# One eight-bank PSUM tile in place of four two-bank tiles, in a kernel with a fixed order of operations

## The chip, the cores and the metric

The kernel runs on one core of one Trainium2 chip. The metric is the device time of one execution in microseconds (us), the median over several executions. A run counts as slow when it is over 1.5% above the fastest of its kernel. The others are called fast, and only those enter ratios. Medians and the ranges behind them are over all runs, slow ones too.

Words used below: PE is the matrix engine, ACT the scalar engine, DVE the vector engine, POOL the general-purpose engine, SP the engine that issues most loads. PSUM is the memory that PE writes its results to; this kernel uses all of it, as eight banks of 512 fp32 values per partition. ACT and DVE empty ("evacuate") those banks.

## The reference

```python
# attention over 8 batches x 8 heads, 576 positions, head size 64
scores = q @ k.T / sqrt(64)          # heads 0-3: the last 32 positions; heads 4-7: every 4th of the last 128
attn   = softmax(where(mask, scores, -1e9)) @ v
x      = heads side by side          # [8, 576, 512]
# channel mix
x_prev = x shifted by one position
xk, xr = mu_k*x + (1-mu_k)*x_prev,  mu_r*x + (1-mu_r)*x_prev
k      = relu(xk @ w_k)              # [.., 1024]
out    = sigmoid(xr @ w_r) * (k*k @ w_v)
```

All inputs and the output are float32; the kernel computes in fp16 with fp32 sums in PSUM.

## The kernel before

The kernel plans itself in Python. It lists its operations (one operation is, for example, the four matmuls of one accumulation), simulates them with rough costs, and records the order that came out. Each engine then runs that fixed order. The planner also assigns the PSUM banks, and it takes the eight banks as independent of each other:

```python
P = Plan(pools, {"pa": OPTIONS["pa"], "p1": OPTIONS["p1"], "cm": OPTIONS["cm"], ...})
OPTIONS = dict(..., pa=[(0, 1), (2, 3), (4, 5)],    # attention: scores and outputs, a pair of banks each
               p1=[(0,), (1,), (2,), (3,)],         # attention: transposes, one bank each
               cm=[(4,), (5,), (6,), (7,)], ...)    # channel mix: one bank for each accumulation
```

The planner does not write semaphores. A layer below it looks at which tiles an instruction reads and writes and puts in the waits. What it sees of PSUM is this:

```python
PA = many(4, [128, 2, 512], FP32, "PA", psp)        # four tiles of two banks

def first(x):
    return P.cells[x.pool][x.idx][0][1]             # number of the first bank that the planner chose

def bank(x):
    return PA[first(x) // 2][:, first(x) % 2]

def banks(x):
    return PA[first(x) // 2]
```

Two parts of the channel mix (cut):

```python
# pk_ops: k = relu(xk @ w_k), one 128-wide slice f at a time, in one bank pk of pool "cm"
nc.tensor.matmul(out=o, lhsT=wk[:, c, f * 128:f * 128 + 128], rhs=XK[:, c, :, a0:a0 + 128],   # L801, 4 of these
                 start=(c == 0), stop=(c == 3))
nc.scalar.activation(out=KR[...], in_=view(), func=AF.Relu, scale=0.5 ** 0.5)                 # L805, evacuates pk
nc.vector.tensor_tensor(out=K2[...], in0=KR[...], in1=KR[...], op=ALU.mult)                   # L815
...
# pv_ops: two more banks, pr and pv
nc.tensor.matmul(out=view(pr)[:, g], lhsT=XR[...], rhs=wr[:, c], ...)                         # L844, 4 of these
nc.scalar.activation(out=TH[...], in_=view(pr), func=AF.Tanh, scale=0.5)                      # L847, evacuates pr
nc.tensor.matmul(out=view(pv)[:, g], lhsT=K2[...], rhs=wv[:, f], ...)                         # L853, 2 times 4 of these
nc.vector.scalar_tensor_tensor(out=OT[...], in0=TH[...], scalar=1.0, in1=view(pv), ...)       # L857, evacuates pv
```

In the attention part, L494 and L522 are transposes of the inputs, L563 and L614 scores, L585 and L635 outputs, and L597, L647 and L704 transposes of the normalised outputs.

The softmax here doesn't subtract the row's maximum and nothing guards it: scores larger than these inputs give would overflow.

Of the kernel before, what the change touches and what calls it, by code (L numbers as in the profile page):

```python
# [9 lines left out]
FP32 = mybir.dt.float32  # L10
# [176 lines left out]
def kernel(  # L187
# [23 lines left out]
    psp = ctx.enter_context(tc.tile_pool(name="psp", bufs=1, space=PSUM))  # L211
# [7 lines left out]
    def many(n, shape, dt, name, pool=const):  # L219
        return [pool.tile(shape, dt, name=f"{name}{i}") for i in range(n)]  # L220
# [31 lines left out]
    M0 = const.tile([128, 8, 96], FP16, name="M0")  # L252
    MB = const.tile([128, 160], FP16, name="MB")
    MB0 = const.tile([128, 2, 96], FP16, name="MB0")
    PA = many(4, [128, 2, 512], FP32, "PA", psp)

    def buf(pool, turn=None):
        return Buf(pool, turn)
# [1 line left out]
    def first(x):  # L260
        return P.cells[x.pool][x.idx][0][1]

    def bank(x):
        return PA[first(x) // 2][:, first(x) % 2]

    def banks(x):
        return PA[first(x) // 2]


    def setup_pool():  # L270
# [22 lines left out]
    def mask_mm(ps, n, rhs):  # L293

        w = math.prod(rhs.shape[1:])
        for par in range(2):
            nc.tensor.matmul(out=banks(ps)[0:n, par, 0:w], lhsT=ident[:, 0:n], rhs=rhs, start=True, stop=False)  # L297
# [38 lines left out]
    def turn_mu():  # L336
        for i in range(2):
            nc.tensor.transpose(out=bank(mub)[:, 4 * i:4 * i + 4], in_=mu[:, i], identity=id4)

    def fix_mu():  # L340
        nc.vector.tensor_scalar(out=nm, in0=bank(mub)[:, 0:8], scalar1=-1.0, scalar2=None, op0=ALU.add)
# [126 lines left out]
    def attention(b, A):  # L468
# [16 lines left out]
        def pt(i, hp):  # L485
            pa = buf(one)

            def tv():
                return bank(pa).bitcast(FP16)[:, 0:576].rearrange("p (y x) -> p y x", y=9)

            def mm():
                for y in range(9):
                    for e in range(2):
                        nc.tensor.transpose(out=tv()[64 * e:64 * e + 64, y], in_=QP[bq.idx][64 * e:64 * e + 64, i, hp, 64 * y:64 * y + 64],  # L494
                                            identity=ident[64 * e:64 * e + 64, 64 * e:64 * e + 64], tile_position=(64 * e, 64 * e))

            m = P.op("PE", 9 * 0.038, mm, dep=[L["p", i], ident_op] + (XREADY[0][0][OPT['hold']] if b == 1 and OPT['hold'] is not None else []), use=[pa, bq, qt], prio=nxt(), warm=False)
            T = (QT, KT)[i]
            QTR[i, hp] = flex(576, ("ACT", "DVE") if b == 0 else ("ACT",),
                              lambda: T[qt.idx][:, hp, 32 * i:].rearrange("p (x y) -> p x y", y=9), lambda: tv().rearrange("p y x -> p x y"),  # L500
                              dep=[m], use=[pa, qt], prio=nxt())
# [44 lines left out]
        def view_o(g):  # L546
            return lambda po: banks(po)[:, 0:g, 0:260].rearrange("p w (h d) -> p w h d", d=65)

        def plain(j):
            ps, at = buf(two), buf("at")  # L550

            def s_mm():
                t = banks(ps)
                if pm:
                    mask_mm(ps, 128, (MB0 if j == 0 else MB[:, 32:128].unsqueeze(1).to_broadcast([128, 2, 96])).unsqueeze(2)
                            .to_broadcast([128, 2, 2, 96]))
                for wl in range(2):
                    w = 2 * j + wl
                    for hp in range(2):
                        for par in range(2):  # L560
                            e = par * 64
                            o = wl * 192 + hp * 96
                            nc.tensor.matmul(out=t[:, par, o:o + 96], lhsT=KT[qt.idx][e:e + 64, hp, 96 * w:96 * w + 128],  # L563
                                             rhs=QT[qt.idx][e:e + 64, hp, 96 * w:96 * w + 96],
                                             start=not pm, stop=not pm or wl + hp == 2)
# [322 lines left out]
    for b in range(1, B):  # L888
# [4 lines left out]
        def en(x):  # L893
            return {"P": ("POOL",), "D": ("DVE",), "A": ("ACT",), "*": ANY, "PA": ("POOL", "ACT"), "PD": ("POOL", "DVE")}[o["e" + x]]
        if o["p"]:
# [59 lines left out]
```

## Time and profile before

| | before |
|---|---|
| time when predicted | 273.19 us median of 3 (272.81 to 277.19) |
| span of the profiled run | 276.7 us (a slow run, granted clock 0.951) |
| PE / DVE / ACT / POOL busy | 238.7 / 182.2 / 153.8 / 74.2 us |
| 720 large matmuls, 215 ns apart when they stream | 155 us |

The page of the profile, its first and fourth part (busy times with shares of the span; the chain that ended last, by engine), and two lines of its fifth (busy time, mean length in ns, then idle time of PE just before and what ended most of it):

```profile
span 276.7 us, 6139 instructions
...
PE 238.7 (86%) x2442; PEld 123.7 (45%) x2442; DVE 182.2 (66%) x361; ACT 153.8 (56%) x255; POOL 74.2 (27%) x93
...
PE 68%; DVE 16%; ACT 9%; issue 3%; DMA 2%; SPq 0%; DVEq 0%; ACTq 0%
...
L801 PE MATMUL PA<-XK,wk 128*128 128x512 f16 x288 | 72.7, 392 | 7.0 <-ACT KR L805 3.9
L853 PE MATMUL PA<-wv,K 128*128 128x512 f16 x288 | 72.8, 389 | 6.7 <-ACT TH L847 4.0
```

No engine is full. PE leads, but "busy 86%" flatters it: the end of a matmul in the profile is modelled, and a large one is drawn as 379 ns long although the next starts 215 ns after it in a stream. For every matmul I take the time to the next one's start and subtract what is usual for its kind (the 20th percentile of its line). The sum of what is left is called PE's **standstill** here: 82.6 us in this run.

What PE and its two helpers wait for, from the view of waits (engine and instruction, then what it waited for: us in total, times, longest):

```profile
ACT KR L805 <- PE PA L801: 33.2, 42, 3.0
DVE K L815 <- ACT KR L805: 25.6, 23, 2.8
...
ACT TH L847 <- PE PA L844: 19.8, 13, 2.1
...
DVE OT L857 <- PE PA L853: 18.0, 13, 2.0
...
ACT TH L847 <- DVE OT L857: 9.6, 8, 2.7
ACT TH L847 <- PE PA L853: 7.5, 7, 2.1
...
DVE OT L857 <- PE PA L844: 4.3, 4, 1.6
...
PE PA L853 <- ACT TH L847: 4.0, 7, 0.7
PE PA L801 <- ACT KR L805: 3.9, 9, 0.7
```

Some of these lines are natural, at least in part: the relu L805 reads what L801 wrote. Others should surprise. The tanh L847 reads bank pr, which L844 wrote. It shares no data with L853, which writes pv, yet it waited 7.5 us for it. It waited 9.6 us for L857, and L853 in turn waited for the tanh. Such waits can be true: L857 reads what a tanh wrote, and there are only two TH buffers to write to; L853 may take over a bank that a tanh has emptied.

The timeline shows one such place closely (start, duration, engine, line, operation; in brackets the idle time before it and what ended that):

```profile
216.39 1.03 PE L801 MATMUL PA<-XK,wk 128*128 128x512 f16 x4
...
217.50 1.02 PE L801 MATMUL PA<-XK,wk 128*128 128x512 f16 x4
...
218.53 1.03 PE L801 MATMUL PA<-XK,wk 128*128 128x512 f16 x4
218.56 1.64 ACT L805 ACTIVATE KR<-PA 128x512 f16<-128x512 f32 x3 [2.70 <-PE PA L801]
```

The first four matmuls fill bank 7 and end at 217.42 (the banks are read from the built program). ACT is idle, and the relu of bank 7 takes 0.60 us, but it starts at 218.56, right after the *second* four end at 218.52, and those write bank 6. Three relus then run in a row. The built programs say why. They list, for each instruction, the semaphore values that it waits for; here the values are translated to the instructions that set them:

```
before  relu of bank 7 waits for: DVE L815 (its output buffer), the last matmul into bank 6
after   relu of bank 7 waits for: DVE L815 (its output buffer), the last matmul into bank 7
```

### The profile page before, as it was taken

What the parts mean: (1) busy time and instruction counts of PE and PEld (TensorE: products, weight loads), DVE (VectorE), ACT (ScalarE), POOL (GpSimd) and SP (SyncE); (2) the same over time, 40 slices, a digit from 0 to 9 for tenths busy, and PEclk for the clock granted to TensorE, in tenths of its full rate; (3) what the DMA queues carried; (4) which work ended last, traced back from release to release, by engine and by line L of the source; (5) the groups of instructions that cost most, each with busy time, mean ns of one, the idle gap of its engine ahead of it and who ended that gap; (6) DMA issues with size and microseconds to landing.
All of it is one profiled execution on the core that took longest, in us unless ns stands there. A gap on an engine that the chain in (4) does not pass through costs nothing.

```text
span 276.7 us, 6139 instructions
## 1 busy us (share of the span) xinstructions
PE 238.7 (86%) x2442; PEld 123.7 (45%) x2442; DVE 182.2 (66%) x361; ACT 153.8 (56%) x255; POOL 74.2 (27%) x93
## 2 busy tenths in 40 slices
PE   1967898699898889978699999978888999999993
PEld 1544255354454445435344455534433554444441
DVE  7676555886864869797657777967576887323221
ACT  2555477583566477667248664766476555644210
POOL 4022575363442317156222344320000000000000
PEclk9985599979999999999689999999999999999999
DMA  7999999999699989599837899861102022111231
GB/s 227 282 239 351 296 217 304 196 238 219 197 247 191 307 183 261 163 261 252 212 121 174 247 242 277 186 146 38 40 0 77 2 76 78 38 39 38 79 114 76
DMA packets 66397, 47.92 MB, mean 173 GB/s; under 512 B 40760, under 2 KB 57152, under 8 KB 66368
## 3 DMA queue, kind: packets, MB, share of 16 engines
q1 hardware_dynamic: 64784, 45.96, 66.3%
q0 software_dynamic: 1584, 1.57, 3.4%
q8 instruction: 19, 0.31, 0.5%
q14 instruction: 10, 0.08, 0.1%
HBM read 36.11 MB, written 9.44 MB: 165 GB/s over the span
## 4 chain that ended last, share of the span: by engine, by line
PE 68%; DVE 16%; ACT 9%; issue 3%; DMA 2%; SPq 0%; DVEq 0%; ACTq 0%
PE PA L853 22%; PE PA L801 21%; PE PA L844 10%; ACT KR L805 4%; DVE OT L857 3%; PE PA L494 3%; PE PA L297 3%; DVE XS L537 2%; PE PA L563 2%; ACT TH L847 2%; DMA ST<-in_q_dram 2%; DVE K L815 1%; DVE XT L350 1%; PE PA L597 1%; DVE AT L625 1%
## 5 line engine op out<-in xcount | busy, mean ns | idle before, releaser
L801 PE MATMUL PA<-XK,wk 128*128 128x512 f16 x288 | 72.7, 392 | 7.0 <-ACT KR L805 3.9
L853 PE MATMUL PA<-wv,K 128*128 128x512 f16 x288 | 72.8, 389 | 6.7 <-ACT TH L847 4.0
L805 ACT ACTIVATE KR<-PA 128x512 f16<-128x512 f32 x72 | 41.1, 597 | 38.6 <-PE PA L801 33.2
L857 DVE SCALAR_TENSOR_TENSOR OT<-TH,PA 128x512 f32<-128x512 f32 x36 | 24.7, 687 | 36.5 <-PE PA L853 18.0
L815 DVE TENSOR_TENSOR K<-KR 128x1024 f16<-128x1024 f16 x36 | 29.0, 808 | 25.6 <-ACT KR L805 25.6
L853 PEld LDWEIGHTS <-K 128*128 128x128 f16 x288 | 27.3, 99 | 38.9 <-issue 11.6
L847 ACT ACTIVATE TH<-PA 128x512 f32<-128x512 f32 x36 | 21.4, 596 | 39.7 <-PE PA L844 19.8
L801 PEld LDWEIGHTS <-wk 128*128 128x128 f16 x288 | 26.9, 99 | 36.8 <-issue 11.1
L844 PE MATMUL PA<-wr,XR 128*128 128x512 f16 x144 | 36.9, 379 | 0.1
L537 DVE TENSOR_TENSOR XS<-PA,RC 96x512 f16<-96x512 f32 (+2 forms) x48 | 30.9, 644 | 1.5
L348 POOL CAST QD<-ST 128x1024 f16<-128x1024 f32 (+1 forms) x21 | 19.8, 955 | 44.5 <-DMA ST<-in_k_dram 22.6
L348 POOL CAST VD<-ST 112x1024 f16<-112x1024 f32 (+1 forms) x16 | 18.0, 1134 | 17.8 <-DMA ST<-in_v_dram 16.3
L346 ACT ACTIVATE XT<-PA 128x384 f16<-128x384 f16 (+2 forms) x22 | 10.5, 486 | 19.2 <-PE PA L704 6.9
L348 POOL CAST QP<-ST 128x1152 f16<-128x1152 f32 x14 | 16.2, 1161 | 17.5 <-DMA ST<-in_q_dram 10.1
L568 ACT ACTIVATE AT<-PA 128x768 f16<-128x768 f32 x24 | 18.6, 811 | 4.2 <-PE PA L563 3.4
L494 PE MATMUL PA<-ident,QP 64*64 64x64 f16 x576 | 14.4, 206 | 7.1 <-DVE QP L350 5.8
L348 POOL CAST VP<-SV 128x512 f16<-128x512 f32 x21 | 14.0, 701 | 21.0 <-DMA SV<-in_v_dram 11.6
L844 PEld LDWEIGHTS <-XR 128*128 128x128 f16 x144 | 13.2, 98 | 14.1
L350 DVE COPY XT<-PA 128x384 f16<-128x384 f16 (+2 forms) x26 | 11.6, 449 | 10.9 <-PE PA L597 4.8
L494 PEld LDWEIGHTS <-QP 64*64 64x64 f16 x576 | 12.6, 120 | 11.3 <-DVE QP L350 5.9
L739 ACT ACTIVATE XR<-DX,nm 128x576 f16<-128x576 f16 (+2 forms) x23 | 15.5, 697 | 0.0
L533 DVE RECIPROCAL RC<-PA 96x8 f32<-96x8 f32 (+2 forms) x48 | 8.9, 185 | 9.8 <-PE PA L585 6.3
(77 smaller groups left out, 272.8 us busy)
## 6 DMA issues: line engine op xcount, KB each, us to landing
SV<-in_v_dram SPq DMA_DIRECT2D x8, 736.0 KB, 6.8
ST<-in_k_dram SPq DMA_DIRECT2D x8, 576.0 KB, 5.8
ST<-in_q_dram SPq DMA_DIRECT2D x8, 576.0 KB, 5.4
ST<-in_k_dram SPq DMA_DIRECT2D x8, 512.0 KB, 5.8
ST<-in_q_dram SPq DMA_DIRECT2D x8, 512.0 KB, 5.6
ST<-in_v_dram SPq DMA_DIRECT2D x8, 448.0 KB, 5.2
ST<-in_v_dram SPq DMA_DIRECT2D x8, 256.0 KB, 5.4
ST<-in_moe_w_k_dram SPq DMA_DIRECT2D x4, 512.0 KB, 6.8
```

The costliest lines, as they stand in the source:

```text
L348: nc.gpsimd.tensor_copy(out=o, in_=i)
L494: nc.tensor.transpose(out=tv()[64 * e:64 * e + 64, y], in_=QP[bq.idx][64 * e:64 * e + 64, i, hp, 64 * y:64 * y + 64], identity=ident[64 * ...
L537: nc.vector.tensor_tensor(out=XS[xs.idx][0:n, 0:g].rearrange("p w (h d) -> p w h d", h=4), in0=fin(po)[0:n, :, :, 0:64], in1=RC[rc.idx][0: ...
L568: nc.scalar.activation(out=AT[at.idx][:, :, 0:96].rearrange("p (a g) c -> p a g c", a=2), in_=banks(ps)[:, :, 0:384].rearrange("p a (g c) ...
L739: nc.scalar.activation(out=d, in_=x, func=AF.Copy, scale=mu[:, c:c + 1])
L801: nc.tensor.matmul(out=o, lhsT=wk[:, c, f * 128:f * 128 + 128], rhs=XK[:, c, :, a0:a0 + 128], start=(c == 0), stop=(c == 3))
L805: nc.scalar.activation(out=KR[kr.idx][:, g0:g0 + G], in_=view(), func=AF.Relu, scale=0.5 ** 0.5)
L815: nc.vector.tensor_tensor(out=K2[k2.idx][:, 2 * f2:2 * f2 + 2], in0=KR[kr.idx], in1=KR[kr.idx], op=ALU.mult)
L844: nc.tensor.matmul(out=view(pr)[:, g], lhsT=XR[:, c, rr[g], a:a + 128], rhs=wr[:, c], start=(c == 0), stop=(c == 3))
L847: nc.scalar.activation(out=TH[th.idx][:, 0:m], in_=view(pr), func=AF.Tanh, scale=0.5)
L853: nc.tensor.matmul(out=view(pv)[:, g], lhsT=K2[k2.idx][:, f, 128 * rr[g]:128 * rr[g] + 128], rhs=wv[:, f], start=(f == 0), stop=(f == NF - 1))
L857: nc.vector.scalar_tensor_tensor(out=OT[ot.idx][:, 0:m], in0=TH[th.idx][:, 0:m], scalar=1.0, in1=view(pv), op0=ALU.add, op1=ALU.mult)
```

## The change

The intent is to describe PSUM to the layer below as what it is, eight banks in one memory, without touching any operation, its place in the order or its bank.

```diff
-    PA = many(4, [128, 2, 512], FP32, "PA", psp)
+    PA = psp.tile([128, 8, 512], FP32, name="PA")
 ...
     def bank(x):
-        return PA[first(x) // 2][:, first(x) % 2]
+        return PA[:, first(x)]

     def banks(x):
-        return PA[first(x) // 2]
+        return PA[:, first(x):first(x) + 2]
```

That is all of it. The two programs have the same instructions in the same order on every engine; what differs is waits and the wait-only instructions that carry some of them.

## The prediction

> **What bounds the kernel.** PE's order of work. The chain of waits runs 68% through PE, 16% DVE, 9% ACT, 2% DMA. The 720 large matmuls start 215 ns apart when they stream (start times in the trace): 155 us of a 276.7 us span. The small matmuls take some 49 us (start-to-start times, summed). "PE busy 86%" counts modelled ends; by start times PE stands still for about 70 us. The page's DMA row is at 9 tenths for most of the first 120 us, but DMA ends few waits on the chain.
>
> **What the change does.** I compared the two built programs. Every engine runs the same instructions in the same order; only semaphore waits differ. Before, 236 waits hold an instruction on one bank for one that touched only the *other* bank of its tile. With one eight-bank tile they go: waits between PE, ACT and DVE are then nearly all between instructions that share a bank or an SBUF tile. (A two-bank tile is tracked as a whole, an eight-bank tile by bank: read from the waits; I don't know why.) Followed through chains of waits, no instruction has to wait for anything later than before. ACT gets 27 more wait-only instructions (89 to 116), while it is idle.
>
> The hardware needs no more: the Trainium skill, "PSUM — Partial Sum Buffer", section "PSUM bank collisions raise a hardware error", asks for semaphores by bank (or bank and quadrant). Its "Perfetto Trace Analysis", section "Matmuls", wants independent groups to rotate through banks so that the evacuation of one overlaps the next group. That overlap is partly lost now: PE writes bank 7 from 216.39 to 217.42 us, its neighbour bank 6 from 217.50 to 218.53, and ACT's 0.60 us relu of bank 7 starts only at 218.56, after 2.70 us idle.
>
> **Cost.** Time by which a neighbour-bank wait outlasted everything the new program still waits for: PE 17.6 us (53 instructions), ACT 32.9 us (43), DVE 12.5 us (20). Only PE's lies directly on the critical path; the others lengthen PE's later waits. I re-timed the trace by arithmetic: each instruction's measured duration, measured semaphore latencies (37 ns PE to ACT or DVE, 52 ns back), new waits for old. With each load's measured time to landing kept, the span shrinks by 24.0 us; with loads queued one after another, so that DMA goes no faster than now, by 20.3 us. In that second case 8 us are won by 105 us, 10 by 160, 19 by 215; the last 60 us (channel mix alone, 32 matmuls in 7.24 us) gain 1 us.
>
> **Prediction:** 252 us (7.8% less), 80% range 246 to 260. Faster by over 2%: 0.95; within 2%: 0.04; slower: 0.01.
>
> **What should show.** Instruction counts equal; busy times of DVE (182) and ACT (154) within 2%. In "who waited for whom", ACT relu L805 for PE L801 falls from 33.2 us to about 20; tanh L847 for DVE L857 (9.6) and for PE L853 (7.5) nearly vanish, and DVE L857 for PE L844 (4.3). PE idles less than 7.0 and 6.7 us before L801 and L853. The tail after attention keeps its length.
>
> **What would make it wrong.** If DMA is already the pacer up to 180 us, waits turn into waits for loads and the gain is 8 to 15 us. PE's granted clock, 0.62 from 20 to 40 us: denser work may lift it (more gain) or lower it. The profiled run was slow (276.7 against 272.8 at best), so fast runs may gain some us less.

## The result

| | before | after |
|---|---|---|
| time | 274.43 us median of 4 (272.81 to 277.19) | 250.24 us median of 4 (249.08 to 252.48) |
| ratio of fast runs | | 0.9146 (95%: 0.9035 to 0.9258) |
| profiled span, state, granted clock | 276.7 us, slow, 0.951 | 250.8 us, fast, 0.965 |
| PE's standstill | 82.6 us | 55.8 us |

A ratio compares the fast runs of the two kernels in the same rounds, so it is not quite the ratio of the medians in the table; the means of the fast runs differ by 23.4 us. E2 below gives a fast profile with the old waits (271.7 us).

The page, the same parts and lines as before:

```profile
span 250.8 us, 6168 instructions
...
PE 227.9 (91%) x2442; PEld 119.5 (48%) x2442; DVE 186.1 (74%) x361; ACT 155.4 (62%) x255; POOL 78.9 (31%) x93
...
PE 72%; DVE 12%; DMA 7%; SPq 2%; issue 2%; POOL 2%; ACT 1%; DVEq 0%; POOLq 0%
...
L853 PE MATMUL PA<-wv,K 128*128 128x512 f16 x288 | 70.5, 383 | 0.0
L801 PE MATMUL PA<-XK,wk 128*128 128x512 f16 x288 | 70.4, 385 | 1.3 <-DVE OT L857 1.0
```

The 29 added instructions are wait-only ones (27 on ACT, 2 on DVE), which the first line counts and the second does not. The work is the same; the span is not.

The view of waits:

```profile
ACT KR L805 <- PE PA L801: 27.9, 52, 4.2
ACT TH L847 <- PE PA L844: 25.7, 24, 2.0
DVE OT L857 <- PE PA L853: 18.1, 15, 2.3
...
DVE K L815 <- ACT KR L805: 15.5, 15, 2.5
...
PE PA L801 <- DVE OT L857: 1.0, 1, 1.0
```

The surprising lines are gone: tanh for L857, tanh for L853, L857 for L844, and both waits of PE for ACT. What remains are true waits: of an evacuation for the matmuls that fill its own bank, of L815 for the relus that it reads, and one of L801 for L857. This change cannot take them away.

The same stretch of work in the timeline of after. PE's groups are spaced as before; ACT's relus now follow their own groups:

```profile
191.95 1.03 PE L801 MATMUL PA<-XK,wk 128*128 128x512 f16 x4
...
193.02 0.60 ACT L805 ACTIVATE KR<-PA 128x512 f16<-128x512 f32 x1 [1.16 <-PE PA L801]
...
193.06 1.02 PE L801 MATMUL PA<-XK,wk 128*128 128x512 f16 x4
...
194.10 1.03 PE L801 MATMUL PA<-XK,wk 128*128 128x512 f16 x4
194.19 0.60 ACT L805 ACTIVATE KR<-PA 128x512 f16<-128x512 f32 x1 [0.57 <-PE PA L801]
```

Bank 7 is full at 192.98 and its relu starts at 193.02. Before, the same relu started 1.14 us after its bank was full.

Where the 26 us between the two profiled spans come from, by the place in PE's order (times of the same matmul in both traces, from each one's first instruction): 3 us are won by 33 us of the old span, 9 by 106, 18 by 160, 24 by 215 and 26 at the end. But the old trace is a slow run, and part of this is its state: between 120 and 140 us, where it records 6.8 us at half the clock and neither E2's fast profile nor that of after has any, 5.8 us are won. Against E2's fast profile of the old waits it is 2 us by 33, 7 by 106, 12 by 160, 19 by 215 and 21 at the end. The last 56 us of the old trace, where the channel mix runs almost alone, became 1.5 us shorter (against E2: 1.8).

### The profile page after: what moved, and what is told of

Same layout as the page of the kernel before. It is cut to its first block, busy times and chain, and to the rows that moved or that the text cites. A ratio compares the mean times of both kernels' runs of the same rounds, so it can differ in the third digit from the quotient of the medians.

```text
span 250.8 us, 6168 instructions
## 1 busy us (share of the span) xinstructions
PE 227.9 (91%) x2442; PEld 119.5 (48%) x2442; DVE 186.1 (74%) x361; ACT 155.4 (62%) x255; POOL 78.9 (31%) x93
## 4 chain that ended last, share of the span: by engine, by line
PE 72%; DVE 12%; DMA 7%; SPq 2%; issue 2%; POOL 2%; ACT 1%; DVEq 0%; POOLq 0%
PE PA L853 24%; PE PA L801 21%; PE PA L844 11%; DMA ST<-in_moe_w_k_dram 5%; PE PA L494 3%; PE PA L563 2%; SPq L430 2%; DVE K L815 2%; DMA ST<-in_k_dram 2%; PE PA L585 2%; PE PA L297 2%; PE PA L647 1%; DVE AT L574 1%; DVE AT L625 1%; DVE XS L537 1%
## 5 line engine op out<-in xcount | busy, mean ns | idle before, releaser
L801 PE MATMUL PA<-XK,wk 128*128 128x512 f16 x288 | 70.4, 385 | 1.3 <-DVE OT L857 1.0
L853 PE MATMUL PA<-wv,K 128*128 128x512 f16 x288 | 70.5, 383 | 0.0
L805 ACT ACTIVATE KR<-PA 128x512 f16<-128x512 f32 x72 | 42.7, 598 | 28.3 <-PE PA L801 27.9
L857 DVE SCALAR_TENSOR_TENSOR OT<-TH,PA 128x512 f32<-128x512 f32 x36 | 24.7, 685 | 22.5 <-PE PA L853 18.1
L853 PEld LDWEIGHTS <-K 128*128 128x128 f16 x288 | 26.4, 98 | 29.4 <-issue 0.6
L801 PEld LDWEIGHTS <-wk 128*128 128x128 f16 x288 | 25.9, 99 | 29.1 <-issue 3.7
L815 DVE TENSOR_TENSOR K<-KR 128x1024 f16<-128x1024 f16 x36 | 27.9, 776 | 15.8 <-ACT KR L805 15.5
L847 ACT ACTIVATE TH<-PA 128x512 f32<-128x512 f32 x36 | 21.5, 597 | 27.0 <-PE PA L844 25.7
L844 PE MATMUL PA<-wr,XR 128*128 128x512 f16 x144 | 36.9, 380 | 0.0
L348 POOL CAST QD<-ST 128x1024 f16<-128x1024 f32 (+1 forms) x21 | 20.7, 998 | 28.4 <-DMA ST<-in_k_dram 17.0
L348 POOL CAST QP<-ST 128x1152 f16<-128x1152 f32 x14 | 17.9, 1280 | 18.2 <-DMA ST<-in_k_dram 7.1
L348 POOL CAST VP<-SV 128x512 f16<-128x512 f32 x21 | 16.2, 804 | 19.2 <-DMA SV<-in_v_dram 10.8
L844 PEld LDWEIGHTS <-XR 128*128 128x128 f16 x144 | 13.1, 98 | 14.0
L745 DVE TENSOR_TENSOR XR<-XR,XT 128x1152 f16<-128x1152 f16 (+2 forms) x18 | 15.8, 891 | 0.3
(77 smaller groups left out, 271.7 us busy)
```

What stands on the lines that cost most here:

```text
L348: nc.gpsimd.tensor_copy(out=o, in_=i)
L745: nc.vector.tensor_tensor(out=t, in0=t, in1=XT[xT.idx][:, c0:c1, :, 2 + o:2 + o + n], op=ALU.add)
L805: nc.scalar.activation(out=KR[kr.idx][:, g0:g0 + G], in_=view(), func=AF.Relu, scale=0.5 ** 0.5)
L815: nc.vector.tensor_tensor(out=K2[k2.idx][:, 2 * f2:2 * f2 + 2], in0=KR[kr.idx], in1=KR[kr.idx], op=ALU.mult)
L844: nc.tensor.matmul(out=view(pr)[:, g], lhsT=XR[:, c, rr[g], a:a + 128], rhs=wr[:, c], start=(c == 0), stop=(c == 3))
L847: nc.scalar.activation(out=TH[th.idx][:, 0:m], in_=view(pr), func=AF.Tanh, scale=0.5)
```

## Experiments

The theory, W: the gain comes from taking away waits between different banks, and from nothing else. Rival L (layout): one large tile gives better addresses or access patterns, and the instructions or the memory get faster. Rival C (clock): PE's granted clock, 0.951 against 0.965, makes the difference. Some expectations quote a "re-timing": durations, latencies and load times as measured in a trace, put together again with the waits of another program.

### E1: two tiles of four banks

```diff
-    PA = many(4, [128, 2, 512], FP32, "PA", psp)
+    PA = many(2, [128, 4, 512], FP32, "PA", psp)
 ...
-        return PA[first(x) // 2][:, first(x) % 2]
+        return PA[first(x) // 4][:, first(x) % 4]
 ...
-        return PA[first(x) // 2]
+        return PA[first(x) // 4][:, first(x) % 4:first(x) % 4 + 2]
```

> PSUM as two tiles of four banks. In the built program each of these tiles is tracked as a whole too: 472 waits are for an instruction on another bank of the same tile (206 with tiles of two, none with one of eight). Theory W (waits): the time follows these waits and not the size of the tile, so it gets far worse than before; re-timing the trace of before with these waits gives 377 us, that of the changed kernel 372. Expected 375, 350 to 400. Rival L (layout: fewer, larger tiles give better addresses or access patterns): between the two kernels, 250 to 275. Rival C (granted clock alone makes the difference): about 275, with the clock of before.

Measured: 405.14 us (402.71 to 406.44), ratio to before 1.4742 (1.4609 to 1.4874). Half-way to one tile is not half-way to the gain; it costs 47%. Rivals L and C fall, since neither went beyond about 275 us. Theory W has the direction and most of the size, but the value is 5 us above its range. In the timeline of this run, one relu's bank and the next group's bank lie in one tile, so PE and ACT take turns:

```profile
330.01 1.02 PE L801 MATMUL PA<-XK,wk 128*128 128x512 f16 x4 [0.83 <-DVE OT L857]
...
331.07 0.60 ACT L805 ACTIVATE KR<-PA 128x512 f16<-128x512 f32 x1 [3.83 <-PE PA L801]
331.72 1.02 PE L801 MATMUL PA<-XK,wk 128*128 128x512 f16 x4 [0.69 <-ACT KR L805]
...
332.78 0.60 ACT L805 ACTIVATE KR<-PA 128x512 f16<-128x512 f32 x1 [1.11 <-PE PA L801]
...
333.43 0.81 PE L801 MATMUL PA<-XK,wk 128*128 128x512 f16 x3 [0.69 <-ACT KR L805]
```

A group of four starts every 1.71 us, while four matmuls streaming at 215 ns need 0.86 us. The missing 28 us may lie in the clock: the trace records 55.7 us at half the clock, as against 28.6 before, and the re-timing kept the clock of the trace it came from. By an estimate from these two figures, 27 us more at half the clock cost at most 14 us, so at least half of the 28 stays unexplained. That was not tested.

### E2: one tile, the waits put back

To each operation that touches PSUM, once it is issued, a by-hand dependency is added on the last operation of each other engine that touched the neighbour bank (0 and 1, 2 and 3, 4 and 5, 6 and 7; cut):

```diff
+    def neighbours(o, first_ins, last_ins):
+        mine = touched(o)                       # the banks of this operation
+        if KEEP(o, mine):                       # here: always
+            for e, name in {(e, name) for x in mine for e, name in seen.get(x ^ 1, {}).items() if e != o.eng}:
+                tc.add_manual_dep(first_ins, name, info, reason="neighbour bank")
+        for x in mine:
+            seen.setdefault(x, {})[o.eng] = last_ins.name
```

> The changed kernel with its one tile of eight banks, and every wait for the neighbour bank put back by hand (banks 0-1, 2-3, 4-5, 6-7), 1439 waits in all as against 1438 before. On PE they land on the weight load in place of the matmul, a little earlier in the queue, which re-timing puts at 4 to 5 us. Theory W: 277 us (re-timed 276.9 from the trace of after, 279.8 from that of before), range 270 to 284, so as slow as before or slightly slower. Rival L: 250, since the tile is that of the changed kernel. Rival C: says nothing about waits; 250 if the clock stays at about 0.965.

Measured: 273.62 us (273.37 to 276.19), ratio to before 0.9984 (0.989 to 1.0078). The layout is that of the changed kernel and the time is that of the old one. This is the run that decides against L. (A recount from the built programs found 227 direct waits between engines that have the neighbour bank as their only reason in the kernel before, 227 in E2 and none after.) Nor do the instructions get faster: the relu L805 takes 597 ns before, 598 after and 597 in E2, L857 687, 685 and 686. E2 also decides against C: its profiled run had a clock of 0.967 and 20.1 us at half the clock, against 0.965 and 19.5 us after, and it still took 271.7 us. Other runs say the same: one run of the kernel before, beside E11, had a clock of 0.987 and took 271.12 us; one of the changed kernel had 0.962 and took 249.08. Its waits are those of before:

```profile
ACT TH L847 <- DVE OT L857: 9.6, 8, 2.7
...
ACT TH L847 <- PE PA L853: 6.6, 7, 1.8
...
PE PA L853 <- ACT TH L847: 4.0, 7, 0.7
PE PA L801 <- ACT KR L805: 3.8, 9, 0.7
```

The 4 to 5 us that the by-hand waits were expected to cost, because they sit on the weight load, did not show.

### E3 and E4: the waits put back on one side

```diff
-KEEP = lambda o, banks: True
+KEEP = lambda o, banks: o.eng == "PE"           # E3
+KEEP = lambda o, banks: o.eng != "PE"           # E4
```

> The changed kernel with the neighbour waits put back on PE alone (PE waits for ACT or DVE reading the neighbour bank). Theory W with both directions mattering: re-timed 257 (from after) to 259 (from before), range 253 to 263. If, as the prediction said, only PE's 17.6 us lie directly on the critical path and the rest merely lengthens PE's waits, this run and the next differ little and their losses add up to less than or about the whole loss. Rival L: 250.

> The changed kernel with the neighbour waits put back on ACT and DVE alone (the reader waits until PE has finished the neighbour bank). PE is never held by a neighbour bank here. Theory W: re-timed 258 (from after) to 260 (from before), range 254 to 264: late evacuation reaches PE through its true waits. A rival form of W, that waits off PE are harmless: 250 to 252. Rival L: 250.

Measured: E3 257.52 us (254.88 to 260.62), ratio 0.9345 (0.9237 to 0.9453). E4 258.37 us (257.36 to 261.08), ratio 0.9426 (0.9309 to 0.9544). Both values lie within a microsecond of the re-timings from the trace of after. (E3's 260.62 is a slow run.) Taken against the changed kernel's 0.9146, PE's waits alone cost 2.0% of the old time and those of ACT and DVE alone 2.8%. Together they cost 8.4% (E2), so more than their sum. That fits a picture of two engines taking turns: a late evacuation harms only if the next matmul must wait for it. No run shows this picture directly beyond these sums and E1's timeline, so it is argued, not shown.

The form of W in which waits off PE are harmless falls with E4. PE is never held there by a neighbour bank, and it still loses.

PE's standstill in the profiled runs, with the span (half-clock: time that the trace records at a clock of 0.5):

| run | span | standstill | span less standstill | half-clock |
|---|---|---|---|---|
| before (slow run) | 276.7 | 82.6 | 194.1 | 28.6 |
| after | 250.8 | 55.8 | 195.0 | 19.5 |
| E1, tiles of four | 401.0 | 206.2 | 194.8 | 55.7 |
| E2, all waits back | 271.7 | 77.1 | 194.6 | 20.1 |
| E3, PE's back | 253.1 | 58.8 | 194.3 | 17.0 |
| E4, ACT's and DVE's back | 256.9 | 63.0 | 193.9 | 15.8 |

The fourth column hardly moves. That is nearly so by definition, since the standstill is what start-to-start times leave over the usual ones, and the kernels have the same matmuls. What it does show is that the usual ones stayed the same: no kernel here streams its matmuls faster or slower, which speaks against L. The gain lies in the gaps, and why a gap was there the table does not say. (Matmuls that ran at half the clock count as standstill too.)

### E5 and E6: the waits put back by bank

```diff
-KEEP = lambda o, banks: True
+KEEP = lambda o, banks: min(banks) >= 4         # E5
+KEEP = lambda o, banks: max(banks) < 4          # E6
```

> The changed kernel with the neighbour waits put back only for operations on banks 4 to 7: the channel mix (one bank each) and the last pair of the attention's score and output tiles. Theory W, that the gain comes from the channel mix's rotation through four banks: re-timed from the trace of after 272.4, from that of before 276; the by-hand waits cost a little more than the old ones, and the run with all of them came 3 us under its re-timing, so expected 269, 262 to 275. Rival: the gain comes mostly from the attention's transposes in banks 0 to 3, then 255 or less here.

> The same for operations that touch only banks 0 to 3: the attention's transposes (one bank each) and its score and output tiles (two banks, whose pair is one unit in either kernel, so no wait is false among themselves). Theory W: re-timed 252.7 from after, 254 to 256 from before; expected 252.5, 250 to 256, so under 2% lost. Rival (attention's banks carry the gain): 262 or more.

Measured: E5 271.22 us (269.8 to 272.34), ratio 0.9862 (0.9789 to 0.9935), inside its expectation. E6 254.66 us (249.53 to 255.91) without a ratio. Three of E6's four runs (254.35 to 255.91) lie over 1.5% above the fourth and count as slow by that rule, so its loss of 0 to 2% against the changed kernel is inconclusive in size. The split is clear all the same: the waits on banks 4 to 7 carry about 7.2 of the 8.5 points (0.9862 less 0.9146; each has an interval of about one point either way). There the channel mix rotates single-bank accumulations, and each one has a neighbour in use. In banks 0 to 3 only the attention's transposes use single banks.

### E7 and E8: are the loads the pace?

The prediction's main doubt was DMA. The page shows its row at 9 tenths for most of the first 120 us before, and for longer after. Both kernels were run with the plain V loads cut, with a wrong result:

```diff
-                eng.dma_start(out=dst(b)[:, 1:24], in_=bass.AP(v.tensor, a.offset, [[D, 128], [96 * D, 23], [1, D]]))
+                eng.dma_start(out=dst(b)[:, 1:7], in_=bass.AP(v.tensor, a.offset, [[D, 128], [96 * D, 6], [1, D]]))
 ...
-        nc.vector.memset(SV[0:32, 0], 0.0)
+        nc.gpsimd.memset(SV, 0.0)
```

> Wrong result on purpose: the changed kernel with the plain V loads cut from 23 windows to 6 (0.74 MB to 0.2 MB a batch, 12% of all bytes read and about 17000 of the 66000 packets); the rest of its staging tile is zeroed once. If loads set the pace of the changed kernel while they last (to about 165 us), it gains 10 us or more over the changed kernel: 240 or less. If they do not, it stays at 246 to 251. I expect 246: the DMA row reads 1.0 to 1.15 until 160 us, but the re-timing that held landing times fixed was the one that came true.

> Wrong result on purpose: the same cut in the kernel before. Theory W (neighbour waits pace it, not loads): 271 to 276, within 2% of before. If loads paced it: 265 or less.

Measured: E7 250.18 us (249.1 to 252.54), ratio 0.9111 (0.9034 to 0.9188), as fast as the changed kernel; it stayed inside the range for loads that set no pace, but did not reach the 246 that was expected. E8 274.22 us (273.72 to 275.68), ratio 0.9982 (0.9912 to 1.0052). The amount of these loads sets neither kernel's pace; the q and k loads were not cut. The windows view shows how fast loads can go here. Its rows give, for a stretch of the span, busy time and count of PE, PEld, DVE, ACT and POOL, then granted clock, DMA share and GB/s. Before:

```profile
120.00:140.00 20.00, 15.38 (x175) 7.95 (x173) 15.04 (x26) 9.47 (x18) 10.70 (x12) 0.85 0.92 219
140.00:160.00 20.00, 18.75 (x198) 9.36 (x196) 14.06 (x31) 14.09 (x26) 5.13 (x8) 0.98 0.74 202
```

After:

```profile
120.00:140.00 20.00, 19.69 (x216) 9.59 (x213) 16.06 (x39) 14.30 (x27) 8.03 (x7) 1.00 0.99 236
140.00:160.00 20.00, 19.33 (x259) 10.82 (x258) 17.59 (x33) 12.10 (x21) 11.14 (x10) 1.00 1.15 258
```

Where PE works faster, the loads do too: from 140 to 160 us DMA moves 258 GB/s where it moved 202 (220 in E2's fast profile), and over the first 160 us 258 as against 234 (241 in E2). That buffers come free earlier would explain it; no run tests this. The two traces are at different places of their work in one window. A DMA share near 1 was no limit here. The Trainium skill, "Perfetto Trace Analysis", section "Identifying the Most-Contended Engine", calls DMA occupancy misleading because there are 16 DMA engines: in the trace of after the share is 1.06 at 291 GB/s from 20 to 40 us, and higher, 1.15, at only 258 GB/s from 140 to 160.

### E9, E10 and E11: a new order

The planner takes the banks as independent, and with the eight-bank tile the program does too. Some of its settings may therefore have been chosen to suit waits that are now gone. Two of its orders were tried with the eight-bank tile, and one of them again with tiles of two:

```diff
 E9   -backlog=3.0, xe=0, ed='P'                 +backlog=4.0, xe=1, ed='PD'
 E10  -sk=('DVE','ACT'), ed='P'                  +sk=('ACT',), ed='PD'
 E11  as E10, with PA as four tiles of two banks
```

> The changed kernel with three settings of its planner changed (loads may be issued 4 in place of 3 us ahead, the attention's last copies on ACT alone, the casts of the dilated q and k on POOL or DVE): the order of operations differs. The planner takes banks as independent, which the program now does too, so its own reckoning should rank orders better than before; it puts this order 1.4% ahead of the changed kernel's. Theory: 244 to 250, within 2% of the changed kernel, perhaps a little faster. Rival: the planner's reckoning is no guide at this size, 250 to 256.

> The changed kernel with two settings of its planner changed (the scaling of one of the two mixed inputs on ACT alone, the casts of the dilated q and k on POOL or DVE). The planner's reckoning puts it 1.0% ahead of the changed kernel's order. Expected 245 to 251; the same two theories as for the run before it.

> The order of e10 with PSUM as four tiles of two banks, as in the kernel before. If the new order is worth what it was worth with one tile (2.8% less than the changed kernel), this comes to about 267 us. If the false waits hide such gains, it stays within 2% of before, 269 to 279. It cannot come near 244 if the neighbour waits are what costs.

Measured: E9 252.18 us (250.63 to 253.76), ratio 0.919 (0.9106 to 0.9274), no gain over the changed kernel and above the 244 to 250 that was expected. E10 244.08 us (242.9 to 248.19), ratio 0.889 (0.8803 to 0.8977), with correct results, just below its 245 to 251. It beats both kernels, the changed one by 2.8% (0.889 over 0.9146). E11, the same order with tiles of two banks: 277.89 us (275.0 to 278.73), ratio 1.0137 (1.0018 to 1.0255).

So the order that is best with one tile is, if anything, worse than the old one with four (by less than 2%), and the change to PSUM is worth 12% in it (0.889 over 1.0137). In the waits of E11 the tanh waits 23.6 us for DVE, where before it waited 9.6:

```profile
ACT TH L847 <- DVE OT L857: 23.6, 15, 2.3
...
DVE OT L857 <- PE PA L844: 19.9, 12, 2.3
```

The planner's own reckoning put E9 ahead of E10 and the chip did not. Which of E10's two settings did it was not tried. Nor was the clock kept out: E10's trace has 8.0 us at half the clock, that of after 19.5, and by an estimate from these the difference can be worth up to 6 us, about the whole gain. Against this stands one pair of runs at nearly the same clock: 244.08 us at 0.976 (E10) and 249.24 at 0.975 (after).

## Why the prediction was right

- **The mechanism was right.** The waits between different banks, counted in the built programs, account for the difference: putting them back returns the old time within about 1% (E2), more of them costs more (E1), and fewer cost less (E3 to E6). The prediction's count of 236 takes waits that the changed program no longer implies, directly or through others. E1's count of 206 takes only direct waits whose source touched just the other bank of the same tile. The recount of 227 follows the rule given under E2. The three are not to be compared with each other.
- **The size.** 252 was predicted and 250.24 measured. The two re-timings gave 24.0 us (each load's time to landing as in the trace) and 20.3 us (DMA no faster than now). Which of them was nearer is open. The medians differ by 24.2 us and the fast runs by 23.4, but the fast profiles of E2 and of after by 20.9 (the fastest of E2's four runs and the slowest of after's). The second version's course, 10 us won by 160 us and 19 by 215, is missed by the slow profile (18 and 24) and nearly met by the fast one (12 and 19). Its premise did not hold: DMA did go faster, 258 GB/s over the first 160 us as against 241 in E2. So if its sum came close, that was partly luck.
- **PE's waits and the others.** The prediction called only PE's 17.6 us directly critical and said that the others lengthen PE's waits. E3 and E4 weigh the two: 2.0% and 2.8% alone, 8.4% together. So PE's waits alone cost some 5.5 us (2.0% of 274), not 17.6, and the other engines' waits matter as much as PE's own.
- **PE before L801 and L853** idled 1.3 and 0.0 us, where it had idled 7.0 and 6.7. Right.
- **Waits that should vanish** (tanh for L857 and L853, L857 for L844) vanished. Right. The relu's wait for L801 fell only from 33.2 to 27.9 us, not to about 20, and the tanh's wait for L844 rose from 19.8 to 25.7. When the wrong waits go, the right ones remain and show in their place, and an evacuation that keeps up with PE waits for PE more often (52 times as against 42). The prediction forgot this.
- **Busy times within 2%.** ACT yes (153.8 and 155.4), DVE just not (182.2 and 186.1). Nothing hangs on it.
- **The tail keeps its length.** Right: it lost 1.5 us of 56.
- **The clock.** Half-clock time was lower after (19.5 as against 28.6 us), but the profile of before was a slow run. E2 had 20.1 us and the old time, so the clock is not where the gain came from. It is where some of the 26 us between the two profiled spans came from.
- **Why a tile of two or four banks is tracked as a whole and one of eight bank by bank** was open in the prediction and still is. A program with a tile of two and one of six banks was built too, not run, and the tile of six was also tracked as a whole (a second build shows the same). Of the sizes looked at, only the one that covers all of PSUM was tracked by bank.

What the hardware asks for was taken from the Trainium skill, "PSUM — Partial Sum Buffer", section "PSUM bank collisions raise a hardware error": semaphores by bank, or by bank and quadrant. Runs with waits by bank alone are correct (E9 and E10, with the tile of the changed kernel). "Perfetto Trace Analysis", section "Matmuls", says that independent groups should rotate through banks so that the evacuation of one overlaps the next group. This kernel did rotate, and still lost the overlap in places that were worth 8.5% of its time.

## What to carry to other kernels

Rotating through PSUM banks is worth what the waits allow, so look up in the built program what each evacuation waits for, and not only in the source which bank it reads. A line in the view of waits that joins two instructions with no data in common (here the tanh's wait for L853, with which it shares only a tile) is worth more attention than a longer line that joins a producer and its reader. After such a fix, tune the order again: the best order under false waits need not be the best without them.

## What the Trainium skill lacked or had wrong

- "PSUM — Partial Sum Buffer" gives the rule of waits by bank, but neither it nor any other page read for this says that the layer which places waits may treat a tile of several banks as one thing. Here that cost 24 us of 274 with tiles of two banks and 155 us of 405 with tiles of four, against one tile of eight (250 us).
- "Perfetto Trace Analysis", section "Matmul Optimizations", advises to see that all 8 banks are in use. It does not add that this is not enough: all eight were in use here at 250, 274 and 405 us alike. Which waits join the banks made the difference.
- "TensorE: Matmul & The Clock Gate", section "Back-to-back issue gap", gives about 131 ns per matmul for a sustained stream with 512 columns and calls the single gap of about 216 ns too high for that case. The page contradicts itself here: its section "Step-by-step: what each phase is for" gives about 216 ns for back-to-back matmuls. In this trace, streams of up to 32 such matmuls, each with its weight load, start 215 to 216 ns apart at full clock (1st percentile and median of the start-to-start times within L844: 215 and 216 ns; 32 of L801 in 6.91 us after).
